# Row sums of the softmax: the two half sums added on VectorE for ten of sixteen head pairs, and the division moved one pair later

## The chip, the cores and the metric

One NeuronCore of a Trainium2 chip runs the whole program in one launch. The metric is the device time of one execution in microseconds (us). The kernel before took 799.79 us (median of three runs, 799.49 to 800.53). Below, PE is TensorE, DVE is VectorE, ACT is ScalarE, POOL is GpSimd and SP is SyncE.

## What is computed

Attention with cluster routing feeds an MLP mixer. There are 4 batches, 8 heads, 768 tokens and a head width of 64. A query sees only the keys that fall in the same of 16 clusters:

```python
mask = q_assign[:, :, :, None] == k_assign[:, :, None, :]
scores = np.where(mask, scale * (q @ k.T), -1e9)
attn = np.exp(scores - max(scores))
attn = attn / (np.sum(attn, axis=-1, keepdims=True) + 1e-09)
x = attn @ v                                    # then heads side by side: (4, 768, 512)
h = np.maximum(xt @ w_tok1, 0.0) @ w_tok2       # over tokens, xt = x transposed
u = x + h.transpose(0, 2, 1)
h2 = np.maximum(u @ w_ch1, 0.0) @ w_ch2         # over channels
return u + h2
```

The change concerns the sum in the fourth line and the division by it.

## The kernel before

All arithmetic is fp32. The kernel runs three stages one after the other.

**Attention** goes over 16 units; unit (or pair) `m` is two heads of one batch, `b, hp = divmod(m, 4)`. In each unit PE does, in the order in which `pair` (L1283) calls for it:

- `scores(m)`: twelve chunks. A chunk is 128 keys by 384 queries for both heads; it fills two PSUM banks, and the chunks use the bank pairs 0-1, 2-3 and 4-5 in turn. The mask is added as a second, bf16 matmul. ACT takes the exponential of each chunk (L1191) into one of seven buffers `exs`; a unit uses six, one for each block of 128 keys.
- `values(m, i)` for the six key blocks: exponentials times V, in 32 matmul instructions each, summed up in banks 6 and 7.
- `route(m + 2, 0)` before `values(m, 4)`: cluster scores of the unit after next, into bank 0. DVE turns them (L1086), takes maxima, compares and turns them back (L1091); ACT makes the mask rows of it (L1095).
- `sums(m, 5)` before the last `values`: a matmul with a matrix of ones adds the exponentials over the keys. Its two passes `n` read `es[0]` and `es[1]` and add up in bank 5.

DVE has made `es[0]` and `es[1]` at the end of `scores`: each is the sum of three exponential buffers, in two additions of 128x1536 elements (`tt`, L881). After the unit, `finish_x` (L1247) turns the denominators out of bank 5 (L1250), clips them (L1252), takes the reciprocal (L1259), turns the result out of banks 6 and 7 into `x` (L1264) and multiplies `x` by the reciprocals (L881, 128x768).

Beside this, DVE prepares the mixer's weights in 31 pieces (`weight_round`, L1307, five instructions each; and the combinations `sub1`, `sub2` after every second piece). The pieces are needed only later and are fitted in where DVE has room. ACT also splits q and k into halves for a DMA transpose and joins them (L871).

**The token stage** multiplies by `w_tok1` and `w_tok2`; ACT copies and DMA transposes bring `x` into the layout `u` (`x_into_u`). **The channel stage** multiplies by `w_ch1` and `w_ch2` for two groups of two batches; each step of three matmuls is followed by an addition out of PSUM on DVE.

The order of the work is made when the program is built. `Program.add` records every operation with what it reads and writes. `Program.plan` then hands operations to the engines by assumed costs (`COST`, and numbers at each call) and due times that are counted back from the PE order. PE's own order is the order of the calls; the other engines' orders come out of the plan. On the chip each engine runs its list in that fixed order and waits on semaphores.

Of the kernel before, what the change touches and what calls it, by code (L numbers as in the profile page):

```python
# [14 lines left out]
ALU = mybir.AluOpType  # L15
# [3 lines left out]
B, H, S, D = 4, 8, 768, 64  # L19
C = 16  # L20
P = 128
NJ = S // P
# [8 lines left out]
HS = HJ * P  # L31
# [14 lines left out]
NP = NG // 2  # L46
NU = 2 * NP
W = 64
SUM_LO, SUM_HI = 1e-15, 1e15
GRAIN = 32  # L50

COST = {
    "ACT": (0.09, 0.00083),
# [175 lines left out]
class Buf:  # L229
# [17 lines left out]
    def k(self, *parts):  # L247

        out = []
        for lo, hi in parts or ((0, self.words),):  # L250
            out.extend(range((self.off + lo) // GRAIN, -(-(self.off + hi) // GRAIN)))
        return out
# [467 lines left out]
def kernel(  # L720
# [26 lines left out]
    nc = tc.nc  # L747
    g = Program()
# [4 lines left out]
    ps = res.enter_context(tc.tile_pool(name="ps", bufs=1, space=bass.MemoryType.PSUM)).tile(  # L753
        [P, 8, 512], F32, name="ps"
    )
# [9 lines left out]
    def buf(kb, shape, dt=F32):  # L765
        return Buf(arena, int(kb * 256), shape, dt)
# [24 lines left out]
    es = [buf(84 + 6 * i, [2, S]) for i in range(2)]  # L791
# [44 lines left out]
    def bank(*i):  # L836
        return [("ps", n) for n in i]


    def mm(dst, lhsT, rhs, start, stop, cost, rd, wr, pos=None, tr=None):  # L840
        def fn(e):
            nc.tensor.matmul(  # L842
                dst, lhsT=lhsT, rhs=rhs, start=start, stop=stop, tile_position=pos,
                is_transpose=tr, skip_group_check=True,
            )

        return g.add({"PE": cost}, fn, rd, wr, mode=(lhsT.shape[0], lhsT.shape[1]))
# [6 lines left out]
    def cost(kind, n):  # L854
        a, b = COST[kind]
        return a + b * n
# [22 lines left out]
    def tt(dst, a, b, op, n, rd, wr, engines=("DVE",)):  # L879
        def fn(e):  # L880
            (nc.vector if e == "DVE" else nc.gpsimd).tensor_tensor(out=dst, in0=a, in1=b, op=op)  # L881

        return g.add({e: cost(e, n) for e in engines}, fn, rd, wr)
# [10 lines left out]
    def vec(fn, c, rd, wr, early=0.0):  # L894
        return g.add({"DVE": c - 0.08}, lambda e: fn(), rd, wr, early=early)
# [27 lines left out]
    def load_qkr(m, after=0.0):  # L923
        b, hp = divmod(m, H // 2)
        for i, a in ((0, k), (1, q)):
            dma(
                qkr.ap[:, i].rearrange("p h j d -> p h (j d)"),
                a[b, 2 * hp : 2 * hp + 2].rearrange("h (p j) d -> p h (j d)", p=P),
                [], qkr.rows(i, i + 1), 384, 1536, after,
            )  # L930
# [96 lines left out]
    def turn_qk(m, banks):  # L1027
        src, T = qks[m % 2], Ts[m % 3]
        for n, bk in enumerate(banks):
            for i in range(4):  # L1030
                a, j = divmod(4 * n + i, NJ)
                a = 1 - a
                turn(
                    ps[:, bk, i * P : (i + 1) * P],
                    src.ap[:, a, j].rearrange("p h d -> p (h d)"),
                    [("qk", m % 2, a, 0), ("qk", m % 2, a, 1)] + src.rows(a, a + 1), bank(bk),
                )

            copy(
                T.ap[:, 4 * n : 4 * n + 4].rearrange("p a t -> p (a t)"), ps[:, bk], 512,  # L1040
                bank(bk), T.rows(4 * n, 4 * n + 4),
            )
# [103 lines left out]
    unit = {}  # L1146

    def scores(m):
        nonlocal nex
        T, M = Ts[m % 3], Ms[m % 2] if m else M0  # L1150
        st = unit[m] = [exs[(nex + i) % len(exs)] for i in range(NJ)]
        nex += NJ

        def chunk(n):
            return divmod(n, NJ) if m == 0 else divmod(n, 2)[::-1]

        def plain(n):
            u, i = chunk(n)
            s, r0 = n % 3, NJ + HJ * u
            for h in range(2):  # L1160
                hs = slice(64 * h, 64 * h + 64)
                mm(
                    ps[:, 2 * s + h, 0:HS], T.ap[hs, i],
                    T.ap[hs, r0 : r0 + HJ].rearrange("p a t -> p (a t)"), True, False, 0.3225,
                    T.rows(i, i + 1) + T.rows(r0, r0 + HJ), bank(2 * s + h), pos=(64 * h, 0),
                )

        ahead = 3 if m == 0 else 0
        for n in range(ahead):
            plain(n)  # L1170
        if m == 0:
            turn_qk(1, (7, 6, 7))
            load_qkr(3, 26.0)
            route(1, 6)
        for n in range(2 * NJ):
            u, i = chunk(n)
            s = n % 3
            if n >= ahead:
                plain(n)
            for h in range(2):  # L1180
                hs = slice(64 * h, 64 * h + 64)
                mm(
                    ps[:, 2 * s + h, 0:HS], M.ap[hs, 1, i * P : (i + 1) * P],
                    M.ap[hs, 0, u * HS : (u + 1) * HS], False, True, 0.081,
                    [("mask", m % 2, a, c, h) for a, c in ((1, i // HJ), (0, u))] + M.k(),
                    bank(2 * s + h), pos=(64 * h, 0),
                )
            ex = st[i]
            g.add(
                {"ACT": 0.70},  # L1190
                lambda e, ex=ex, s=s, u=u: nc.scalar.activation(  # L1191
                    out=ex.ap[:, :, u * HS : (u + 1) * HS], in_=ps[:, 2 * s : 2 * s + 2, 0:HS],
                    func=ACT.Exp, scale=SM_SCALE,
                ),
                bank(2 * s, 2 * s + 1),
                ex.rows(0, 2, u * HS, (u + 1) * HS) + ([("exps", m)] if n == 2 * NJ - 1 else []),
            )
        for n in range(2):
            a = es[n]
            x, y, z = st[HJ * n : HJ * n + HJ]  # L1200
            tt(a.ap, x.ap, y.ap, ALU.add, 2 * S, x.k() + y.k(), a.k())
            tt(a.ap, a.ap, z.ap, ALU.add, 2 * S, a.k() + z.k(), a.k())

    def mms(parts, cost, rd, wr, mode):

# [9 lines left out]
    def tokens(ap, gr):  # L1215

        return ap.rearrange("p (j t) -> p j t", t=P)[:, :, 32 * gr : 32 * gr + 32]
# [13 lines left out]
        )  # L1231

    def sums(m, bk):
        for n in range(2):
            mms(
                [
                    (
                        ps[32 * gr : 32 * gr + 32, bk, 0:HS], ones.ap,
                        tokens(es[n].ap.rearrange("p h t -> p (h t)"), gr), n == 0, n == 1,
                        (0, 32 * gr),  # L1240
                    )
                    for gr in range(4)
                ],
                0.645, es[n].k() + ones.k(), bank(bk), (P, 32),
            )

    def finish_x(m, bk):  # L1247
        b, hp = divmod(m, H // 2)
        x, rcp = xs[b], rcps[m % 2]
        vec(lambda: nc.vector.transpose(out=denT.ap, in_=ps[:, bk, 0:HS]), 0.57, bank(bk), denT.k())  # L1250
        def den():
            nc.vector.tensor_scalar(  # L1252
                out=dall.ap[:, m].rearrange("p h j -> p (h j)"),
                in0=denT.ap.rearrange("p (n r) -> p n r", r=32)[:, :, 0],
                scalar1=SUM_LO / 2, scalar2=2 * SUM_HI, op0=ALU.max, op1=ALU.min,
            )

        vec(den, 0.2, denT.k(), [("dall", m)])
        vec(lambda: nc.vector.reciprocal(out=rcp.ap, in_=dall.ap[:, m]), 0.2,  # L1259
            [("dall", m)], rcp.k())  # L1260
        cols = slice(hp * P, (hp + 1) * P)
        xk = x.rows(0, NJ, hp * P, (hp + 1) * P)
        vec(
            lambda: nc.vector.transpose(  # L1264
                out=x.ap[:, :, cols].rearrange("p j (c d) -> p c j d", d=32),
                in_=ps[:, 6:8, 0:HS],
            ),
            0.96, bank(6, 7), xk,
        )
        xv = x.ap[:, :, cols].rearrange("p j (h d) -> p j h d", h=2)  # L1270
        tt(
            xv, xv,
            rcp.ap.rearrange("p h j -> p j h").unsqueeze(3).to_broadcast([P, NJ, 2, D]),
            ALU.mult, S, xk + rcp.k(), xk,
        )
# [7 lines left out]
    def pair(m):  # L1283
        scores(m)
        if m >= 1 and m + 2 < NP:
            join_qk(m + 2)
        if m:
            next_qk(m)
        for i in range(NJ):
            if i == 4 and 1 <= m < NP - 2:  # L1290
                route(m + 2, 0)
            if i == NJ - 1:
                sums(m, 5)
            values(m, i)
        finish_x(m, 5)
        if m == 0:
            load_v(2)
            turn_qk(2, (1, 2, 3))
            route(2, 0)
            next_qk(m)  # L1300
        if m + 3 < NP:
            load_v(m + 3)
# [632 lines left out]
    first = token1(0, Tx, w1)  # L1935
# [71 lines left out]
```

## Time and profile before

| | |
|---|---|
| three runs | 799.49, 799.79, 800.53 us; median 799.79 us |
| the profiled execution | 799.38 us; its span from first to last instruction 797.6 us |
| granted TensorE clock | 0.999 of full speed |
| PE busy | 783.8 us (98% of the span) |
| DVE busy | 659.4 us (83%) |
| ACT busy | 469.8 us (59%) |
| POOL busy | 188.8 us (24%) |

How to read it: the attention units fill the span up to about 333 us, the token stage lies between about 333 and 419 us, and the channel stage takes the rest. A row of the timeline names the start in us from the span's start, the length, engine, line and operation, output and input shape, and how many equal neighbours it merges; a bracket gives the idle time of that engine just before and what ended it. In the groups, `x80` is the number of instructions, then come the busy time in us and the mean length of one in ns. A matmul's end is modelled, so for PE the distance between starts says more than the length. In the windows, the columns are busy us of PE, PEld (weight loads), DVE, ACT and POOL with their instructions, the granted clock, the busy share of the DMA engines and GB/s.

### The profile page before, as it was taken

The page shows a single profiled execution, that of the slowest core. Times are in us where ns is not written, and L with a number is a line of the kernel's source. Part 1 is how long each engine was busy: PE and PEld are TensorE (multiplying, and loading weights), DVE is VectorE, ACT ScalarE, POOL GpSimd, SP SyncE. Part 2 cuts the span into 40 slices and gives each one's busy share as a digit, 9 for nine tenths or more (in the row PEclk, how much of TensorE's full clock was granted, in tenths as well). Part 3 has the DMA queues.
Part 4 walks back from the last instruction along what each step waited for, and adds up shares of the span by engine and source line. Part 5 has one row for each costly group of instructions (what it writes and reads, how often), then busy time and mean ns, then how long its engine had stood idle before and what let it go on. Part 6 is the DMA issues. An engine that isn't in the chain of part 4 may idle for free.

```text
span 797.6 us, 15467 instructions
## 1 busy us (share of the span) xinstructions
PE 783.8 (98%) x6063; PEld 466.9 (59%) x6063; DVE 659.4 (83%) x861; ACT 469.8 (59%) x618; POOL 188.8 (24%) x184
## 2 busy tenths in 40 slices
PE   7999999999999999999999999999999999999997
PEld 5566666666666666544555555555555555555554
DVE  6988899999999999999994677899952566799964
ACT  5588888888888875698714568503256104400433
POOL 0000000000000000000353499800186379840000
PEclk9999999999999999999999999999999999999999
DMA  9466779999999985479848787635597433333766
GB/s 213 153 160 167 172 169 229 223 211 215 229 226 237 223 249 134 97 148 211 177 122 274 270 290 265 223 99 144 143 210 195 130 106 102 99 104 105 177 148 154
DMA packets 264881, 143.69 MB, mean 180 GB/s; under 512 B 184160, under 2 KB 260704, under 8 KB 264800
## 3 DMA queue, kind: packets, MB, share of 16 engines
q1 hardware_dynamic: 262432, 141.83, 70.2%
q8 instruction: 50, 0.82, 0.4%
q10 hardware_dynamic: 2368, 0.79, 0.4%
q14 instruction: 31, 0.25, 0.1%
HBM read 91.95 MB, written 28.61 MB: 151 GB/s over the span
## 4 chain that ended last, share of the span: by engine, by line
PE 82%; DVE 11%; ACT 4%; issue 2%; ACTq 0%; DVEq 0%
PE ps L842 65%; PE ps L1208 17%; DVE arena L881 9%; ACT arena L871 3%; ACT arena L861 1%; ACT arena L888 0%; DVE arena L863 0%; DVE arena L1264 0%; DVE arena L1337 0%; ACTq L901 0%; ACT L980 0%; ACT arena L1191 0%; DVE arena L1334 0%; DVE arena L1331 0%; DVE arena L1086 0%
## 5 line engine op out<-in xcount | busy, mean ns | idle before, releaser
L842 PE MATMUL ps<-arena 128*128 128x384 f32 (+5 forms) x2735 | 639.7, 462 | 8.4 <-DVE arena L881 2.1
L842 PEld LDWEIGHTS ps<-arena 128*128 128x128 f32 (+1 forms) x2351 | 341.1, 184 | 252.0 <-issue 62.7
L881 DVE TENSOR_TENSOR arena<-arena 128x1536 f32<-128x1536 f32 (+6 forms) x341 | 354.8, 1063 | 19.8 <-ACT arena L1191 9.0
L881 POOL TENSOR_TENSOR arena<-arena 128x384 f32<-128x384 f32 x178 | 188.1, 1086 | 516.5 <-DVE arena L881 382.4
L881 DVE TENSOR_TENSOR arena<-ps,arena 128x384 f32<-128x384 f32 (+3 forms) x227 | 189.3, 844 | 100.2 <-PE ps L842 90.4
L871 ACT COPY arena<-arena 128x768 uint16<-128x768 uint16 x223 | 192.0, 952 | 58.7 <-DVE arena L881 29.3
L1191 ACT ACTIVATE arena<-ps 128x768 f32<-128x768 f32 x192 | 153.8, 810 | 30.4 <-PE ps L842 29.3
L1208 PE MATMUL ps<-arena 128*32 128x192 f32 (+1 forms) x3328 | 151.1, 339 | 0.0
L1208 PEld LDWEIGHTS ps<-arena 128*32 128x32 f32 x3328 | 106.5, 110 | 48.0 <-issue 18.3
L861 ACT COPY arena<-ps 128x1152 f32<-128x1152 f32 (+2 forms) x45 | 32.8, 738 | 133.7 <-PE ps L842 125.2
L888 ACT ACTIVATE arena<-arena 128x1152 f32<-128x1152 f32 (+1 forms) x38 | 40.0, 1077 | 55.8 <-DVE arena L881 55.3
L1865 ACT ACTIVATE arena<-arena 128x768 f32<-128x768 f32 x40 | 38.5, 967 | 17.3 <-DMA arena<-in_moe_w_ch_dram 17.0
L842 PEld LDWEIGHTS <-arena 64*128 64x128 bf16 x384 | 19.2, 94 | 25.0 <-issue 0.6
L1095 ACT ACTIVATE arena<-arena 128x384 bf16<-128x384 f32 x16 | 11.3, 707 | 16.3 <-issue 9.9
L1331 DVE SCALAR_TENSOR_TENSOR arena<-arena 128x512 uint32<-128x512 uint32 (+1 forms) x31 | 20.5, 667 | 0.5
L1337 DVE SCALAR_TENSOR_TENSOR arena<-arena 128x512 f32<-128x512 uint32 (+1 forms) x31 | 20.3, 666 | 0.5
L1264 DVE STREAM_TRANSPOSE arena<-ps 128x768 f32<-128x768 f32 x16 | 15.6, 974 | 0.6 <-PE ps L1208 0.4
L1327 DVE TENSOR_SCALAR arena<-arena 128x512 uint32<-128x512 uint32 (+1 forms) x31 | 12.6, 406 | 0.3 <-DMA arena<-in_moe_w_ch_dram 0.3
L1334 DVE TENSOR_SCALAR arena<-arena 128x512 uint32<-128x512 uint32 (+1 forms) x31 | 12.3, 409 | 0.4
L1086 DVE STREAM_TRANSPOSE arena<-ps 128x384 f32<-128x384 f32 x16 | 9.2, 575 | 3.0 <-PE ps L842 2.7
L1250 DVE STREAM_TRANSPOSE arena<-ps 128x384 f32<-128x384 f32 x16 | 9.2, 575 | 0.8 <-PE ps L1208 0.6
L1091 DVE STREAM_TRANSPOSE arena<-arena 128x384 f32<-128x384 f32 x16 | 9.3, 578 | 0.6
(58 smaller groups left out, 47.2 us busy)
## 6 DMA issues: line engine op xcount, KB each, us to landing
arena<-wd SPq DMA_DIRECT2D x196, 192.0 KB, 2.4
wd<-arena SPq DMA_DIRECT2D x84, 224.0 KB, 3.6
arena<-in_moe_w_ch_dram SPq DMA_DIRECT2D x48, 256.0 KB, 4.6
arena<-in_moe_w_ch_dram SPq DMA_DIRECT2D x16, 768.0 KB, 5.3
arena<-in_v_dram SPq DMA_DIRECT2D x16, 384.0 KB, 4.8
out_dram<-arena SPq DMA_DIRECT2D x14, 384.0 KB, 4.1
arena<-in_k_dram SPq DMA_DIRECT2D x13, 384.0 KB, 4.0
arena<-in_q_dram SPq DMA_DIRECT2D x13, 384.0 KB, 4.4
```

What stands on the lines that cost most here:

```text
L842: nc.tensor.matmul(dst, lhsT=lhsT, rhs=rhs, start=start, stop=stop, tile_position=pos, is_transpose=tr, skip_group_check=True,)
L861: nc.scalar.copy(out=dst, in_=src)
L871: nc.scalar.copy(out=dst, in_=src)
L881: (nc.vector if e == "DVE" else nc.gpsimd).tensor_tensor(out=dst, in0=a, in1=b, op=op)
L888: nc.scalar.activation(out=dst, in_=src, func=ACT.Relu)
L1191: lambda e, ex=ex, s=s, u=u: nc.scalar.activation(out=ex.ap[:, :, u * HS : (u + 1) * HS], in_=ps[:, 2 * s : 2 * s + 2, 0:HS], func=ACT.Exp ...
L1208: nc.tensor.matmul(dst, lhsT=lhsT, rhs=rhs, start=start, stop=stop, tile_position=pos, skip_group_check=True,)
L1264: lambda: nc.vector.transpose(out=x.ap[:, :, cols].rearrange("p j (c d) -> p c j d", d=32), in_=ps[:, 6:8, 0:HS],),
L1327: vec(lambda: nc.vector.tensor_scalar(out=hh, in0=hi, scalar1=0x07FFFFFF, scalar2=3, op0=ALU.bitwise_and, op1=ALU.logical_shift_left,), f, ...
L1331: vec(lambda: nc.vector.scalar_tensor_tensor(out=TT, in0=hi, scalar=0xC0000000, in1=hh, op0=ALU.bitwise_and, op1=ALU.bitwise_or), 0.14 + 0 ...
L1337: vec(lambda: nc.vector.scalar_tensor_tensor(out=ll, in0=lo, scalar=float(2.0**-52), in1=hh.bitcast(F32), op0=ALU.mult, op1=ALU.mult,), 0. ...
L1865: lambda e, i=i, func=func, bias=bias, n=n, hi=hi: nc.scalar.activation(out=hi, in_=hi, func=func, bias=bias, accum_out=wsum.ap[:, i, n : ...
```

## The change

For the units 1 to 10 (the letters V of `FOLD`) DVE adds `es[0]` to `es[1]` in a fifth addition, and PE multiplies only this one sum by the ones. The other six units keep both halves. The multiplication with ones and the division move for all units: `sums(m - 1)` is now called after `values(m, 0)` of the next unit, with the denominators' part of `finish_x` (turning, clipping, reciprocal, multiplying `x`) behind it. Turning `x` out of banks 6 and 7 stays at the unit's end. The additions `add_up(m)` are called behind `sums(m - 1)`, because they overwrite what that reads. The last unit does both at its end, into bank 4. The branch for `"T"` isn't used.

```diff
+FOLD = "-VVVVVVVVVV-----"
...
+    def add_up(m):
+        st = unit[m]
         for n in range(2):
             a = es[n]
             x, y, z = st[HJ * n : HJ * n + HJ]
             tt(a.ap, x.ap, y.ap, ALU.add, 2 * S, x.k() + y.k(), a.k())
             tt(a.ap, a.ap, z.ap, ALU.add, 2 * S, a.k() + z.k(), a.k())
+        a, b = es[1], es[0]
+        if FOLD[m] == "V":
+            tt(a.ap, a.ap, b.ap, ALU.add, 2 * S, a.k() + b.k(), a.k())
...
     def sums(m, bk):
-        for n in range(2):
+        first = 0 if FOLD[m] == "-" else 1
+        for n in range(first, 2):
...
-                        tokens(es[n].ap.rearrange("p h t -> p (h t)"), gr), n == 0, n == 1,
+                        tokens(es[n].ap.rearrange("p h t -> p (h t)"), gr), n == first, n == 1,
...
-    def finish_x(m, bk):
+    def finish_x(m, bk, part):
...
+        if part == 0:
+            vec(  # transpose of banks 6 and 7 into x
...
+            return
...
         for i in range(NJ):
             if i == 4 and 1 <= m < NP - 2:
                 route(m + 2, 0)
-            if i == NJ - 1:
-                sums(m, 5)
+            if i == 1:
+                if m:
+                    sums(m - 1, 5)
+                    finish_x(m - 1, 5, 1)
+                add_up(m)
+            if i == NJ - 1 and m == NP - 1:
+                sums(m, 4)
             values(m, i)
-        finish_x(m, 5)
+        finish_x(m, 5, 0)
+        if m == NP - 1:
+            finish_x(m, 4, 1)
```

More of the change, by code (lines that the diff above doesn't have):

```diff
@@ L1202, in scores, with fn @@
             tt(a.ap, a.ap, z.ap, ALU.add, 2 * S, a.k() + z.k(), a.k())
+        a, b = es[1], es[0]
+        if FOLD[m] == "V":
+            tt(a.ap, a.ap, b.ap, ALU.add, 2 * S, a.k() + b.k(), a.k())
+        if FOLD[m] != "T":
+            return
+        def fn(e):
+            nc.gpsimd.dma_start(
+                a.ap.rearrange("p h t -> p (h t)"), b.ap.rearrange("p h t -> p (h t)"),
+                accum_op=ALU.add,
+            )
+        g.add({"POOL": 1.0}, fn, a.k() + b.k(), a.k(), (2.2 * 768 * 1024, 6144))
     def mms(parts, cost, rd, wr, mode):
@@ L1245, in sums @@
             )
-    def finish_x(m, bk):
+    def finish_x(m, bk, part):
         b, hp = divmod(m, H // 2)
         x, rcp = xs[b], rcps[m % 2]
+        cols = slice(hp * P, (hp + 1) * P)
+        xk = x.rows(0, NJ, hp * P, (hp + 1) * P)
+        if part == 0:
+            vec(
+                lambda: nc.vector.transpose(
+                    out=x.ap[:, :, cols].rearrange("p j (c d) -> p c j d", d=32),
+                    in_=ps[:, 6:8, 0:HS],
+                ),
+                0.96, bank(6, 7), xk,
+            )
+            return
         vec(lambda: nc.vector.transpose(out=denT.ap, in_=ps[:, bk, 0:HS]), 0.57, bank(bk), denT.k())
@@ L1260, in finish_x @@
             [("dall", m)], rcp.k())
[L1261 to L1269, printed above, removed]
         xv = x.ap[:, :, cols].rearrange("p j (h d) -> p j h d", h=2)
```

## The prediction

> **What bounds the kernel now.** I read the page's first part, then the windows by stage, then the waits, then the timeline of one attention unit.
>
> ```profile
> PE 783.8 (98%) x6063; PEld 466.9 (59%) x6063; DVE 659.4 (83%) x861; ACT 469.8 (59%) x618; POOL 188.8 (24%) x184
> ...
> core 0: us, PE busy (x) PEld busy (x) DVE busy (x) ACT busy (x) POOL busy (x), PEclk, DMA share, GB/s
> 20.00:340.00 320.00, 318.51 (x4585) 198.39 (x4582) 298.25 (x412) 258.10 (x335) 0.00 (x0) 1.00 0.81 193
> 340.00:420.00 80.00, 77.74 (x213) 39.05 (x212) 75.24 (x134) 55.88 (x71) 20.16 (x19) 1.00 0.78 167
> 420.00:520.00 100.00, 100.00 (x312) 58.84 (x311) 67.88 (x60) 62.66 (x101) 70.41 (x68) 1.00 0.77 262
> ...
> PE ps L842 <- DVE arena L881: 2.1, 5, 0.9
> ```
>
> In the attention PE is busy for 318.5 of 320 us, but DVE for 298.3 too: two engines stand at their limit, and the change moves work from one to the other. The waits decide which leads: PE waited for a DVE addition five times in the whole span, 2.1 us together. The unit confirms it.
>
> ```profile
> 176.13 9.96 PE L842 MATMUL ps<-arena 64*128 64x384 f32 x72
> 177.25 9.75 ACT L1191 ACTIVATE arena<-ps 128x768 f32<-128x768 f32 x12 [1.57 <-PE ps L842]
> 186.02 5.41 PE L1208 MATMUL ps<-arena 128*32 128x192 f32 x128
> 191.25 0.83 PE L842 MATMUL ps<-arena 128*32 128x384 f32 x8
> 191.89 4.07 PE L1208 MATMUL ps<-arena 128*32 128x192 f32 x80
> 194.61 0.71 ACT L1095 ACTIVATE arena<-arena 128x384 bf16<-128x384 f32 x1 [0.97 <-ACT arena L871]
> 194.73 0.58 DVE L1250 STREAM_TRANSPOSE arena<-ps 128x384 f32<-128x384 f32 x1 [0.20 <-PE ps L1208]
> 195.89 1.40 PE L842 MATMUL ps<-arena 64*128 64x384 f32 x8
> ```
>
> From start to start: scores 9.89 us, four `values` 5.23 (1.31 each), the route 0.64, then `values`, sums, `values`, and the next unit begins 19.76 us after this one. So PE sets the time, and a PE instruction taken out of a unit counts, if DVE still arrives in time.
>
> **PE's part, the gain.** A half sum has the shape of the route: eight instructions of 32 columns by 384. The route takes 0.64 us from start to start (191.25 to 191.89).
>
> ```profile
> L1208 PE MATMUL ps<-arena 128*32 128x384 f32 x256 | 23.6, 486 | 0.0
> L881 DVE TENSOR_TENSOR arena<-arena 128x1536 f32<-128x1536 f32 x80 | 140.0, 1756 | 13.0 <-ACT arena L1191 9.0 <-DVE arena L881 0.5
> L1331 DVE SCALAR_TENSOR_TENSOR arena<-arena 128x512 uint32<-128x512 uint32 x27 | 18.3, 683 | 0.3
> L1327 DVE TENSOR_SCALAR arena<-arena 128x512 uint32<-128x512 uint32 x27 | 11.2, 414 | 0.3 <-DMA arena<-in_moe_w_ch_dram 0.3
> ```
>
> The 256 instructions are sixteen units of two halves; ten halves go: 10 x 0.64 = **-6.4 us**.
>
> **DVE's part, what is added.** Ten additions of 1.756 us are 17.6 us on an engine that idled 21.7 us in those 320. Work has to give way: in the built order of the changed kernel the weight instructions behind the attention grow from 49 to 70. Does a unit then fit? The fixed work per unit:
>
> ```profile
> 172.42 0.58 DVE L1086 STREAM_TRANSPOSE arena<-ps 128x384 f32<-128x384 f32 x1
> 173.03 0.55 DVE L1087 TENSOR_REDUCE arena<-arena 128x24 f32<-128x384 f32 x1
> 173.62 0.56 DVE L881 TENSOR_TENSOR arena<-arena 128x384 f32<-128x384 f32 x1
> 174.21 0.58 DVE L1091 STREAM_TRANSPOSE arena<-arena 128x384 f32<-128x384 f32 x1
> 174.97 0.58 DVE L1250 STREAM_TRANSPOSE arena<-ps 128x384 f32<-128x384 f32 x1 [0.18 <-PE ps L1208]
> 175.58 0.17 DVE L1252 TENSOR_SCALAR arena<-arena 128x12 f32<-128x12 f32 x1
> 175.79 0.23 DVE L1259 RECIPROCAL arena<-arena 128x12 f32<-128x12 f32 x1
> 175.94 0.63 DVE L1331 SCALAR_TENSOR_TENSOR arena<-arena 128x512 uint32<-128x512 uint32 x1
> 176.48 0.97 DVE L1264 STREAM_TRANSPOSE arena<-ps 128x768 f32<-128x768 f32 x1
> 177.49 0.96 DVE L881 TENSOR_TENSOR arena<-arena 128x768 f32<-128x768 f32 x1
> ```
>
> Route 2.27, finish 2.91, five additions 8.78: 13.96 us. The order puts eight to twelve weight instructions between two routes in units 5 to 11, about ten (fourteen to sixteen before). A piece has two instructions of 0.414, two of 0.683 and an addition that I take like those: 0.58 on average, 5.8 for ten, 19.8 us of durations. Neighbours that don't depend on each other overlap: 175.94 plus 0.63 reaches past 176.48 by 0.09. With ten such pairs 18.9 us remain, against 19.76 - 0.64 = 19.12 on PE. It fits, by 0.2 us.
>
> *The place where DVE could hold PE.* The next unit's scores need bank 0, so the route's first turn must have ended. The order puts in front of it: turning the last unit's denominators, the two additions of `es[1]` (they wait for the sums, whose input they overwrite) and the fold. From the start of the half sum: 0.64, plus 0.26 until DVE starts (sums end at 191.89 + 1.31 + 1.28 = 194.48, DVE starts at 194.73), 0.58, three times 1.756, then the turn 0.58: 7.3 us. PE needs 0.64, three `values` 3.92, route 0.64, two `values` 2.62: 7.8. So 0.5 us of room, less up to 0.68 where a weight instruction stands in between: nothing in units 5 to 11.
>
> Unit 2 is fuller: ten weight instructions and seven large additions, since unit 1's came late. 12.3 + 2.27 + 1.7 (two turns and a clip) + 5.8 - 0.9 = 21.2 us against 19.12, an overhang of 2.1. It starts from a lead: in unit 1 the turn ends after 0.64 + 0.26 + 0.58 + 3 x 1.756 + 0.58 = 7.3 us, and PE needs it after 1.28 + 3.92 + 0.64 + 2.62 = 8.5. So PE waits **+1.0**; bounds 0 and 2.5 (no lead, and the next unit late as well).
>
> **A move the diff doesn't show.** In units 3 to 11 ACT's mask operation (L1095) now stands between the eighth and the ninth exponential; before it stood ahead of all twelve (194.61). Unit 1 of the kernel before has it after the ninth:
>
> ```profile
> 36.23 0.85 PE L842 MATMUL ps<-arena 128*32 128x384 f32 x8 [0.78 <-ACT arena L861]
> ...
> 37.79 9.96 PE L842 MATMUL ps<-arena 64*128 64x384 f32 x72 [0.71 <-DVE arena L1086]
> 38.98 7.19 ACT L1191 ACTIVATE arena<-ps 128x768 f32<-128x768 f32 x9
> 46.07 0.70 ACT L1095 ACTIVATE arena<-arena 128x384 bf16<-128x384 f32 x1
> 46.76 2.24 ACT L1191 ACTIVATE arena<-ps 128x768 f32<-128x768 f32 x3
> 47.68 5.41 PE L1208 MATMUL ps<-arena 128*32 128x192 f32 x128
> ```
>
> There PE went from scores to values in 9.89 us as ever: free. One place earlier, the ninth exponential moves from about 45.4 to 46.05 and ends at 46.9; the twelfth chunk, which needs its banks, would begin at 37.79 + 11 x 0.81 = 46.7. That is 0.2 us, in nine units **+1.8**; bounds 0 and 0.7 each (the whole operation), 6.2.
>
> **Ends.** The third copy of `turn_qk(2)` goes from ACT to DVE, which shortens the 0.78 us that PE waits at 36.23: **-0.3** (0 to -0.6). In the last unit all four additions must follow `sums(14)`: 0.64 + 0.26 + 4 x 1.756 = 7.9 us, and the last half sum is due after 1.28 + 4 x 1.31 + 0.64 = 7.2: **+0.8** (0.3 to 1.6). Multiplying `x` a unit later costs nothing: units 0 to 14 have a unit of cover, and in the last unit the order keeps it where it was.
>
> **Behind the attention.** The token stage begins when the exponentials' buffers are free, and its chain runs over ACT and DVE, so it moves with the attention's end:
>
> ```profile
> 336.31 5.76 ACT L871 COPY arena<-arena 128x768 uint16<-128x768 uint16 x7
> ```
>
> DVE has two more additions of 1.756 and a second finish to do at its start, and ten weight instructions less in all: **+0.3** (-0.5 to +2). Thirty-five weight instructions now stand in the first channel products, where there were four:
>
> ```profile
> 454.66 1.36 DVE L881 TENSOR_TENSOR arena<-ps,arena 128x1152 f32<-128x1152 f32 x1 [0.58 <-PE ps L842]
> ```
>
> An eviction takes 1.36 us and 0.58 are idle, so one instruction of 0.41 to 0.68 fits into most gaps: **0** (up to +3, a tenth of a microsecond for each of the 31 new ones; the gap is the cover).
>
> Sum: -6.4 + 1.0 + 1.8 - 0.3 + 0.8 + 0.3 = **-2.8 us**. From the profiled execution's own 799.38 us (1.8 of them outside the span) this gives 796.6; the median of the three runs, 799.79, lies 0.4 above that execution, so beside the median I predict 797.0.
>
> [...] By the row, PE has 318.5 of 320 us, and its period never waits. [...]
>
> **The rivals.**
>
> 1. *DVE takes the lead* (slower). If the ten weight instructions don't overlap as in the trace, a unit is 19.8 of DVE plus the 0.26 at the handover, 20.06, and more than 19.76 is slower than before: ten units x 0.3 = +3.0, with the tail's 0.8 and the 0.3 behind it 803.9 beside the median. For it: the room of only 0.2 us; against: before, some 28 instructions with the same overlaps ran in 19.76 without a wait. Chance 0.13.
> 2. *The gain is kept whole up to the tail*: the mask operation finds its gap and DVE is on time: 799.8 - 6.4 + 0.8 = 794.2. Chance 0.15.
> 3. *Given back behind the attention*: the weight work pushed out of the attention lands where PE waits. If half of the 35 instructions, each 0.2 too long for its gap, hold an eviction, the channel loses 3.5 us: 797.0 + 3.5 = 800.5. [...] Chance 0.22, a third of it for a loss beyond 801.4.
> 4. *The fold isn't done*: excluded, the ten additions stand in the built order.
>
> **Chances.** The forecast case (795 to 798.2) 0.5, rival 2 0.15, rival 3 0.22, rival 1 0.13. A measurement of this kernel tells a change of about 0.2% (1.6 us) from none: below 798.2 is faster, above 801.4 slower. Faster: 0.50 + 0.15 = 0.65. Same: two thirds of rival 3, 0.15. Slower: the rest of it and rival 1, 0.20. The range goes from 793.3 (rival 2 with the first pair's gain and a little more) to 802.0, which takes in most of rival 3 and leaves out rival 1.
>
> **What would show it.** Right: units 2 to 11 with a period of 19.1 to 19.4 us; L1208 with ten times eight matmuls of 384 columns fewer; ninety 128x1536 additions; a wait of PE for L1191 of about 0.2 us a unit; DVE at 19 of 20 us in the attention. Wrong: a period near 20 with PE waiting for L881 or L1086 (rival 1), or new PE waits between 409 and 460 us (rival 3).

## The result: slower by 1.1%, and the profile after

The changed kernel takes 809.06 us (median; 807.96 to 809.6), the kernel before 800.16 us beside it; the ratio is 1.0111, 95% interval [1.0099, 1.0123]. The forecast was 797.0 us. The profiled execution took 808.78 us with a span of 807.0, against 799.38 and 797.6 before: 9.4 us more. Three of the 84 runs of the kernel before that were taken beside the experiments needed 807.4 to 808.5 us, two of them with a granted clock of 0.994 like the 0.993 of the changed kernel here; no trace of these was kept, so why is open. In the changed kernel most lines are higher by one; the multiplication of the values is L1225 (was L1208), the addition helper L882, the mask operation L1096.

**The attention** did what was predicted. First the groups of the attention, then one unit on PE and ACT, and that unit as a window (columns: busy us of PE, PEld, DVE, ACT, POOL, granted clock, DMA share, GB/s):

```profile
L882 DVE TENSOR_TENSOR arena<-arena 128x1536 f32<-128x1536 f32 x76 | 132.2, 1747 | 11.4 <-PE ps L1225 8.2 <-ACT arena L1192 1.0
L1225 PE MATMUL ps<-arena 128*32 128x384 f32 x176 | 17.4, 487 | 0.5 <-DVE arena L882 0.5
...
172.81 10.16 PE L843 MATMUL ps<-arena 64*128 64x384 f32 x72
173.93 6.52 ACT L1192 ACTIVATE arena<-ps 128x768 f32<-128x768 f32 x8 [2.67 <-PE ps L843]
180.35 0.70 ACT L1096 ACTIVATE arena<-arena 128x384 bf16<-128x384 f32 x1
181.04 2.90 ACT L1192 ACTIVATE arena<-ps 128x768 f32<-128x768 f32 x4
182.90 6.05 PE L1225 MATMUL ps<-arena 128*32 128x192 f32 x136
192.13 10.16 PE L843 MATMUL ps<-arena 64*128 64x384 f32 x72
...
172.81:192.13 19.32, 19.32 (x285) 12.03 (x281) 18.31 (x24) 16.53 (x22) 0.00 (x0) 1.00 0.74 192
```

There are 176 matmuls of 384 columns in place of 256. The unit has 19.32 us in place of 19.76: the half sum's 0.64 is gone, but the scores last 10.09 (172.81 to 182.90) in place of 9.89, because the mask operation now stands between the eighth exponential and the ninth. The end of the attention, and PE's waits from 20 to 330 us and behind that:

```profile
318.60 8.64 PE L1225 MATMUL ps<-arena 128*32 128x192 f32 x184
327.71 2.15 PE L1225 MATMUL ps<-arena 128*32 128x384 f32 x40 [0.47 <-DVE arena L882]
329.80 2.41 PE L843 MATMUL ps<-arena 128*128 128x512 f32 x5
...
PE ps L843 <- DVE arena L864: 0.9, 1, 0.9
PE ps L1225 <- DVE arena L882: 0.5, 1, 0.5
...
PE ps L843 <- issue: 7.6, 1, 7.6
PE ps L843 <- DVE arena L882: 2.2, 4, 1.2
```

The first matmul of the token stage starts at 329.80 us; before it was 332.95. So 3.15 us were won there. From then on I compared the start of the same matmul in both traces, after minus before: -3.5 us at the end of the token stage (419), -3.1 at 447, -2.7 at 462, **+5.1** behind a stall, +7.0 some 4 us later, +7.3 at the last products, and +9.4 at the end of the span. Two places took everything back.

**The stall.** It stands in the first channel products. DVE, POOL and PE there, then the windows (the same columns, PE's granted clock third from the end):

```profile
469.35 1.36 DVE L882 TENSOR_TENSOR arena<-ps,arena 128x1152 f32<-128x1152 f32 x1 [0.58 <-PE ps L843]
470.62 8.83 DVE L882 TENSOR_TENSOR arena<-arena 128x448 f32<-128x448 f32 x1
479.37 2.61 DVE L882 TENSOR_TENSOR arena<-ps,arena 128x1152 f32<-128x1152 f32 x2
...
451.43 27.54 POOL L882 TENSOR_TENSOR arena<-arena 128x384 f32<-128x384 f32 x28 [2.58 <-DVE arena L882]
...
480.82 19.46 PE L843 MATMUL ps<-arena 128*128 128x384 f32 x54 [7.64 <-issue]
...
473.18:477.64 4.46, 0.00 (x0) 0.00 (x0) 4.46 (x1) 0.00 (x0) 4.46 (x6) 1.00 0.05 19
477.64:480.82 3.18, 0.00 (x0) 0.03 (x1) 3.18 (x3) 0.07 (x1) 1.33 (x2) 0.50 0.13 29
480.82:484.47 3.65, 3.65 (x6) 2.12 (x7) 1.16 (x1) 3.65 (x5) 0.00 (x0) 0.50 0.50 112
484.47:490.00 5.53, 5.53 (x18) 3.24 (x18) 3.94 (x3) 4.29 (x6) 1.96 (x2) 1.00 0.61 207
```

One weight combination of 128x448 (`sub2`), which takes 0.62 us in another place (experiment 1), stands on DVE as busy for 8.83 us. It began while POOL ran 28 additions without a gap, and ended 0.5 us after POOL's run did (451.43 + 27.54 = 478.97). The evictions queue behind the combination, and PE stands for 7.64 us. "issue" names nothing there: the wait is for DVE, as the evictions at 479.37 show. The first of these ends at 480.7 (1.34 us), and PE resumes at 480.82. The granted clock falls to 0.50 while PE stands, 4.46 us after its last matmul, and stays there for 3.65 us after PE has resumed. In the kernel before, POOL had a run like it at this place, but DVE had only evictions beside it, each with one input from PSUM, and these weren't disturbed: 1.358 us on average, against 1.357 over the whole span. POOL's row there, and DVE's one group between 454 and 483 us:

```profile
454.16 28.92 POOL L881 TENSOR_TENSOR arena<-arena 128x384 f32<-128x384 f32 x30 [2.26 <-DVE arena L881]
...
L881 DVE TENSOR_TENSOR arena<-ps,arena 128x1152 f32<-128x1152 f32 x16 | 21.7, 1358 | 9.3 <-PE ps L842 9.3
```

**The end of the program.** Behind the last store SP runs a chain of semaphore and drain instructions. The views leave these out; in the trace's records SP stands still in this chain behind its 990th instruction:

```
kernel           SP records   hold in the closing chain that isn't common to all
before              988       none
after               996       1.92 us, behind no. 990
```

The hold accounts for the last 2 us. A transfer of an instruction queue lands in it; but these queues carry ten packets in the last 26 us of the kernel before too, so this alone doesn't show that the transfer is the cause.

### The profile page after: what moved, and what is told of

Same layout as the page of the kernel before. It is cut to its first block, busy times and chain, and to the rows that moved or that the text cites. A ratio compares the mean times of both kernels' runs of the same rounds, so it can differ in the third digit from the quotient of the medians.

```text
span 807.0 us, 15286 instructions
## 1 busy us (share of the span) xinstructions
PE 783.0 (97%) x5983; PEld 465.2 (58%) x5983; DVE 683.9 (85%) x871; ACT 464.7 (58%) x617; POOL 190.4 (24%) x185
## 4 chain that ended last, share of the span: by engine, by line
PE 80%; DVE 10%; ACT 3%; POOL 3%; issue 2%; DVEq 0%; POOLq 0%
PE ps L843 63%; PE ps L1225 17%; DVE arena L882 9%; POOL arena L882 3%; ACT arena L872 3%; ACT arena L862 0%; DVE arena L864 0%; ACT arena L889 0%; DVE arena L1362 0%; DVE arena L1359 0%; DVE arena L1365 0%; ACT arena L1192 0%; DVE arena L1355 0%; DVE arena L1087 0%; POOL arena masks.py:199 0%
## 5 line engine op out<-in xcount | busy, mean ns | idle before, releaser
L882 DVE TENSOR_TENSOR arena<-arena 128x1536 f32<-128x1536 f32 (+6 forms) x350 | 381.0, 1111 | 17.4 <-PE ps L1225 8.2
L882 POOL TENSOR_TENSOR arena<-arena 128x384 f32<-128x384 f32 x179 | 189.7, 1091 | 522.2 <-DVE arena L882 386.4
L882 DVE TENSOR_TENSOR arena<-ps,arena 128x384 f32<-128x384 f32 (+3 forms) x227 | 189.1, 845 | 84.1 <-PE ps L843 80.9
L1192 ACT ACTIVATE arena<-ps 128x768 f32<-128x768 f32 x192 | 150.5, 811 | 36.1 <-PE ps L843 34.5
L1225 PE MATMUL ps<-arena 128*32 128x192 f32 (+1 forms) x3248 | 144.9, 335 | 0.5 <-DVE arena L882 0.5
L1225 PEld LDWEIGHTS ps<-arena 128*32 128x32 f32 x3248 | 103.7, 110 | 45.2 <-issue 13.9
L1096 ACT ACTIVATE arena<-arena 128x384 bf16<-128x384 f32 x16 | 11.2, 701 | 12.0 <-issue 12.0
```

The lines of the kernel that those rows point to most:

```text
L1192: lambda e, ex=ex, s=s, u=u: nc.scalar.activation(out=ex.ap[:, :, u * HS : (u + 1) * HS], in_=ps[:, 2 * s : 2 * s + 2, 0:HS], func=ACT.Exp ...
L1225: nc.tensor.matmul(dst, lhsT=lhsT, rhs=rhs, start=start, stop=stop, tile_position=pos, skip_group_check=True,)
```

## Experiments

All times of "before" are runs beside the kernel in question.

**1. Move the one addition ahead of POOL's run.** A list of moves is applied to the finished order, and an instruction whose inputs aren't there yet is held back:

```diff
+MOVES = [(("sub2", 2, 5, 2), ("sub2", 2, 5, 0))]
...
+        for name, behind in MOVES:
+            at = next(i for i, (o, e) in enumerate(order) if self.names.get(o) == name)
+            item = order.pop(at)
+            to = next(i for i, (o, e) in enumerate(order) if self.names.get(o) == behind)
+            order.insert(to + 1, item)
```

> The changed kernel with one VectorE instruction moved: the last-but-one combination of the last weight round (sub2(2), 128x448, both inputs in SBUF), which stood inside POOL's unbroken run and lasted 8.83 us, stands right behind the first combination of that round, ahead of POOL's run. All else keeps its order. Theory A (one addition with two SBUF inputs is starved by POOL's back-to-back run, and the evictions queue behind it): the addition lasts 0.6 to 1.2 us, the 7.64 us stall of PE at 475 goes, and with it the low clock behind it (some 2 us): 809.1 - 7.8 - 1.9 = 799.4, and 797.3 if the 1.9 us at the program's end go too. Rival B (the evictions or the stores are late for another reason, the weight work in this stage as such): PE still stalls in 460 to 480, 806 to 809.

Measured: 799.42 us, ratio 0.999 [0.998, 0.9999]. The chip gives 9.6 us back for the place of one instruction. The moved combination in its new place; then POOL's run, and PE's waits behind the attention:

```profile
449.83 0.62 DVE L901 TENSOR_TENSOR arena<-arena 128x448 f32<-128x448 f32 x1
...
451.79 29.56 POOL L901 TENSOR_TENSOR arena<-arena 128x384 f32<-128x384 f32 x30 [3.12 <-DVE arena L901]
...
PE ps L862 <- DVE arena L901: 2.2, 4, 1.2
PE ps L862 <- issue: 0.4, 1, 0.4
```

Rival B falls: the other weight instructions stay in this stage, and of PE's waits only 0.4 us are new there ("issue"). The 2 us at the end stay too (1.46 us of hold, again behind SP's 990th instruction), and with what the other weight instructions cost in the channel stage (1.7 us, see below) the attention's gain is just cancelled.

**2 and 3. Put such an instruction into the kernel before.** Same place, once with two SBUF inputs, once with one:

```diff
+        nc.vector.tensor_tensor(out=flat[:, 0:448], in0=flat[:, 512:960], in1=flat[:, 1024:1472], op=ALU.add)
```

```diff
+        nc.vector.reduce_max(out=flat[:, 0:14], in_=flat[:, 512:960].rearrange("p (n c) -> p n c", c=32), axis=AX.X)
```

> The kernel before with one instruction more: a 128x448 addition of two SBUF inputs into a dead buffer, on VectorE, behind the third eviction of the product with index 1 in the first channel products, in the middle of POOL's run of 30 instructions (454 to 483 us); nothing reads its result. Theory A: it lasts until POOL pauses, up to 9 to 12 us, the evictions behind it wait, PE stalls: 808 to 812. Rival B (the addition gets its turn at POOL's next instruction, as the one at 456.87 us of the changed kernel did in 1.15 us, and the harm there came from something else): 800.2 to 801.5.

> The kernel before with another instruction at the same place as in e2_two_inputs: a maximum over 128x448 of one SBUF input into 128x14 of a dead buffer; nothing reads it. Theory A, in the form that two SBUF inputs make the difference: 0.5 us for it, no stall, 800.2 to 800.8. Rival C (any VectorE instruction without a PSUM input is starved there): as long as e2_two_inputs, 808 or more.

Measured: 811.7 us, ratio 1.0145 [1.0128, 1.0162], for the addition; 800.32 us, 0.9998 [0.9978, 1.0018], for the maximum. DVE's rows around the addition with PE's wait, and then the row of the maximum:

```profile
470.24 1.36 DVE L883 TENSOR_TENSOR arena<-ps,arena 128x1152 f32<-128x1152 f32 x1 [0.58 <-PE ps L844]
471.51 10.11 DVE L1651 TENSOR_TENSOR arena<-arena 128x448 f32<-128x448 f32 x1
481.54 2.61 DVE L883 TENSOR_TENSOR arena<-ps,arena 128x1152 f32<-128x1152 f32 x2
...
482.94 9.43 PE L844 MATMUL ps<-arena 128*128 128x384 f32 x23 [8.87 <-DVE arena L883]
...
482.94:486.50 3.56, 3.56 (x6) 2.04 (x7) 1.21 (x1) 3.56 (x5) 0.00 (x0) 0.50 0.22 26
```

```profile
471.72 0.61 DVE L1651 TENSOR_REDUCE arena<-arena 128x14 f32<-128x448 f32 x1
```

One addition makes such a loss, 11.8 us of it, in a kernel without folds: 8.87 us of stall, and the granted clock at 0.50 for 3.56 us behind it. A maximum that reads one SBUF input in the same place is free. It differs from the addition in the operation and in how little it writes too, so the second input alone isn't isolated; and one input isn't safe by itself. In the changed kernel a weight instruction with one SBUF input, 0.42 us elsewhere, took 1.22 beside a single POOL addition, and another 1.00:

```profile
434.10 1.24 POOL L882 TENSOR_TENSOR arena<-arena 128x384 f32<-128x384 f32 x1 [3.33 <-PE ps L843]
434.40 1.22 DVE L1355 TENSOR_SCALAR arena<-arena 128x512 uint32<-128x512 uint32 x1
...
417.20 1.00 DVE L1362 TENSOR_SCALAR arena<-arena 128x512 uint32<-128x512 uint32 x1
```

**4. The deferral alone.** `FOLD = "-" * 16`.

> The changed kernel without a single half sum added on VectorE: all sixteen pairs keep both sums on TensorE, but sums, denominators and multiplication stand a unit later as in the changed kernel. The order puts no weight instruction into POOL's run. Theory A: the units have 19.76 us, no starved addition, 799.5 to 801.0. Rival D (the deferral itself costs in the attention, or shifts the tail and the end of the program): 802 or more; if the hold of 1.9 us at the program's end comes from the longer program text, it is here too, and the sum is 801.5 to 803.

Measured: 800.12 us, ratio 0.9999 [0.999, 1.0009]. One unit:

```profile
155.20 9.96 PE L843 MATMUL ps<-arena 64*128 64x384 f32 x72
165.09 6.70 PE L1225 MATMUL ps<-arena 128*32 128x192 f32 x144
174.97 1.40 PE L843 MATMUL ps<-arena 64*128 64x384 f32 x8
```

19.77 us, as before: adding up, multiplying and scaling one unit later costs nothing and brings nothing. SP has 987 records and no hold.

**5 and 6. The hold at the end.** SP gets drain instructions in the attention, 24 in the kernel of experiment 1, 8 in the kernel before:

```diff
+    def pad(self, e):
+        self.nsp += e == "SP"
+        if e == "SP" and 200 <= self.nsp < 200 + PAD:
+            self.extra()
...
+    g.extra = lambda: nc.sync.drain()
```

> The kernel of e1_ahead with 24 drain instructions more on SyncE, one behind each of its transfers 200 to 223, in the attention, where SyncE has room. Traces so far: in the changed kernel and in e1_ahead SyncE stands still for 1.9 and 1.5 us at the end of the program, both times behind its 990th instruction of the trace (of 996 and 995), with a transfer of instructions landing at that time; before and the others have 987 or 988 and no such hold. Theory E (the program has grown past a limit of what SyncE has at hand there): with 1019 the 990th lies ahead of the wait for the last stores, so the hold goes: 799.4 - 1.9 = 797.5. Rival F (the hold hangs on something else, the last stores or the shape of the tail): 799.0 to 799.8 as e1_ahead.

> The kernel before with 8 drain instructions more on SyncE, one behind each of its transfers 200 to 207, which makes 996 of them, as many as the changed kernel has. Theory E: a hold of about 1.9 us at the end of the program, 801.7 to 802.0. Rival F: 799.9 to 800.3.

Measured: 797.52 us, ratio 0.9965 [0.9951, 0.9979], and 801.75 us, ratio 1.002 [1.0011, 1.003]. SP's records:

```
kernel           SP records   hold in the closing chain
e1_ahead            995       1.46 us, behind no. 990
e5_pad24           1019       none
e6_before_pad8      996       2.23 us, behind no. 990
```

Theory E held in both directions, with the same position each time: the hold went and came with the number of SP's instructions, none at 988 and 1019, 1.46 to 2.23 us at 995 and 996. What ends the hold isn't shown. The change had lengthened SP's program by eight semaphore instructions, to 996; with its 988 the kernel before was two short of the 990th. With 1019, the 990th lies 13.5 us ahead of the end, where SP waits for stores anyway.

**7 and 10. The mask operation.** e7_mask has this line, e10_best the same with 11 in place of 8; both keep the move and the drains of e5_pad24:

```diff
+MOVES += [(("mask", m), ("exp", m - 1, 8)) for m in range(4, 13)]
```

> The kernel of e5_pad24 with ScalarE's mask operation of the pairs 4 to 12 placed behind the ninth exponential of the unit, where it stood before the change in unit 1, in place of between the eighth and the ninth. Theory G (the operation there costs PE 0.2 us a unit): units 3 to 11 have 19.12 us in place of 19.31, 1.7 us less than e5_pad24, 795.8 if that has 797.5. Rival H (the units are held by VectorE, 19 of whose 19.3 us are taken, and the wait only changes its name): less than 0.5 us.

> The kernel of e7_mask with the mask operation of the pairs 4 to 12 behind the twelfth exponential in place of the ninth, ahead of the copies for the next pair. In e7_mask the scores run without a wait (9.89 us), and the units still have 19.21 us and not 19.12. Theory I (the operation, wherever it stands among the exponentials, makes the last ones late for the values, by 0.09 us): 19.12 us a unit, 9 x 0.09 = 0.8 us less than e7_mask, 795.6. Rival H (VectorE holds the unit, or the copies behind it come late): 796.2 to 797, or slower.

Measured: 796.41 us, ratio 0.9951 [0.9935, 0.9968], and 795.98 us, ratio 0.9939 [0.9918, 0.9961]. The unit of the second:

```profile
171.09 9.96 PE L872 MATMUL ps<-arena 64*128 64x384 f32 x72
180.99 6.05 PE L1254 MATMUL ps<-arena 128*32 128x192 f32 x136
190.21 2.21 PE L872 MATMUL ps<-arena 64*128 64x384 f32 x14
```

Scores 9.90 us, unit 19.12: the 0.2 us belonged to the operation, not to DVE, and rival H falls. Behind the ninth exponential half of it came back (units of 19.21 us); behind the twelfth all of it. So e7_mask came 1.1 us below e5_pad24, where 1.7 were expected. e10_best is the fastest of all: the change with two places in the order mended and 24 drains on SP gains 0.6%. Between e7_mask and e10_best the medians differ by 0.4 us where 0.8 were expected, and the intervals overlap.

**8, 11 and 12. When does POOL let such an addition in?** The addition of experiment 2, seven and four evictions earlier, and then in its old place with a POOL instruction that reads its result and so makes POOL pause:

> The kernel before with the same 128x448 addition of two SBUF inputs as in e2_two_inputs, but seven evictions earlier, near the beginning of POOL's run (about 458 us), where POOL follows close behind the evictions that it needs. Theory A: it waits until POOL runs out of work that is ready; POOL's next pieces need evictions that queue behind it, so that comes after 2 to 8 us, and PE stalls by that less 1 us: 802 to 808. Rival B (its turn comes at the next end of a POOL instruction, as for the one at 456.87 us of the changed kernel, 1.15 us): 800.0 to 801.0.

> The kernel before with the 128x448 addition of two SBUF inputs behind the eviction that lies three behind that of e8_early (there it lasted 0.67 us and cost nothing) and four ahead of that of e2_two_inputs (there 10.1 us): at about 464 us, 10 us into POOL's run of 29. Theory J (it is starved where POOL's next pieces have all their inputs and stand ready one behind another, which is so from about 466 us on, when the products that POOL follows have been evicted): here it is still served after one instruction of POOL, 799.7 to 800.5. Rival K (only the first few instructions of POOL's run let it in, by chance): starved until POOL pauses, 15 us or until the evictions that POOL needs are held, 803 or more.

> The kernel of e2_two_inputs, where the 128x448 addition lasted 10.1 us, with one POOL instruction more: a 128x384 addition that reads the result, put behind the first POOL instruction that began after the other one was held (the first difference for the last product, 471.5 to 472.5 us). POOL so has to pause for VectorE one instruction later, in place of going on to 481 us; nothing of the reference reads either result. Theory A (VectorE waits for a pause of POOL and for nothing else): the addition lasts 1.2 to 1.8 us, the evictions behind it come 0.5 to 1 us late, 800.3 to 801.5. Rival L (the addition at that place is slow for a reason of its own, its buffers or a transfer that it waits for): 10 us again, and POOL held with it, 811 or more.

Measured: 799.8 us (ratio 0.9997 [0.9987, 1.0006]), 799.98 us (0.9996 [0.9976, 1.0016]) and 800.7 us (1.0 [0.9977, 1.0023]). The addition in the three, with the POOL instruction behind it in the first and POOL's rows in the last:

```profile
458.11 0.67 DVE L1651 TENSOR_TENSOR arena<-arena 128x448 f32<-128x448 f32 x1
458.25 1.39 POOL L883 TENSOR_TENSOR arena<-arena 128x384 f32<-128x384 f32 x1
```

```profile
463.91 0.63 DVE L1651 TENSOR_TENSOR arena<-arena 128x448 f32<-128x448 f32 x1
```

```profile
472.00 1.53 DVE L1651 TENSOR_TENSOR arena<-arena 128x448 f32<-128x448 f32 x1
...
454.74 18.31 POOL L883 TENSOR_TENSOR arena<-arena 128x384 f32<-128x384 f32 x19 [2.26 <-DVE arena L883]
473.61 1.01 POOL L1654 TENSOR_TENSOR arena<-arena 128x384 f32<-128x384 f32 x1 [0.56 <-DVE arena L1651]
```

My expectation for e8_early was wrong: near the start of the run the addition gets its turn at the next end of a POOL instruction, whose successor then takes 1.39 us in place of 1.0. At 464 us it is the same, as theory J said. At 472 it isn't, unless POOL has to pause: in e12_pool_waits POOL's run ends at 473.05 and the addition at 473.53. So what ended the wait in the late part is shown: a pause of POOL. Why POOL makes room without a pause up to 464 us and not from 470 on is not. Theory J forecast the result at 464 us, but no run isolates it, and POOL's own rows show no difference: its additions start 0.95 to 0.97 us apart ahead of the early additions as ahead of the late ones.

**9. Eight folds in place of ten**, nothing moved by hand: `FOLD = "-VVVVVVVV-------"`, with the 24 drains.

> The changed kernel with half sums added in eight pairs (1 to 8) in place of ten, and with the 24 drain instructions of e5_pad24; no instruction is moved by hand. With two additions less the last weight instruction stands ahead of POOL's run of itself. Theory A: no stall in the channel products; two half sums more on TensorE cost 2 x 0.45 = 0.9 us against e5_pad24, and fewer weight instructions between the evictions give some of the 1.2 us back that it lost there: 797.0 to 798.0. Rival B (the stall belongs to the folding as such): 804 or more.

Measured: 798.65 us, ratio 0.9974 [0.9955, 0.9993]. POOL's run is whole, and PE's waits name no stall:

```profile
451.71 29.01 POOL L890 TENSOR_TENSOR arena<-arena 128x384 f32<-128x384 f32 x30 [2.26 <-DVE arena L890]
...
PE ps L851 <- DVE arena L890: 1.9, 4, 0.8
```

Rival B falls again: eight folds have no stall. The time is 0.65 us above the expected range, and of the profiled execution 3.0 us lie outside its span where the other profiled ones have 1.8 to 2.0 (2.1 to 3.0 in its ten runs); I can't explain that, and whether eight or ten is better isn't told apart here.

## Why the prediction was wrong

The step that failed is the channel stage under "Behind the attention": "so one instruction of 0.41 to 0.68 fits into most gaps", with a term of 0, "up to +3". It measured +10.8. I took an instruction's length from rows where nothing competed with it, and asked only whether it fits into DVE's gap of 0.58 us. Experiments 1 and 2 show what the row beside it, POOL's unbroken 28.92 us, does to an instruction with two SBUF inputs: 10.1 us for 0.6. The other weight instructions stayed inside the bound: e5_pad24, without the stall, loses 1.7 us of its lead in the channel stage.

Rival 3 had the stage right (its sign named waits between 409 and 460 us; the stall begins at 473), and its price of 3.5 us was mis-sized, with the direction turned round: I priced what DVE's weight instructions do to the evictions; what happened is what POOL did to DVE. The trace of before has neighbours to price that by: seven between 391 and 418 us, additions with two SBUF inputs that were 0.4 to 0.8 us longer beside POOL's additions. Two of them, one that ran without POOL beside it, and POOL's rows:

```profile
391.73 1.42 DVE L881 TENSOR_TENSOR arena<-arena 128x512 f32<-128x512 f32 x1
399.72 0.68 DVE L881 TENSOR_TENSOR arena<-arena 128x512 f32<-128x512 f32 x1
414.22 1.31 DVE L881 TENSOR_TENSOR arena<-arena 128x448 f32<-128x448 f32 x1
...
390.33 2.28 POOL L881 TENSOR_TENSOR arena<-arena 128x384 f32<-128x384 f32 x2 [0.30 <-DVE arena L881]
413.62 4.09 POOL L881 TENSOR_TENSOR arena<-arena 128x384 f32<-128x384 f32 x3 [0.85 <-PE ps L842]
```

These rows showed the direction before the change was run: POOL held DVE (1.42 us in the first against 0.68 in the second, which ran alone). They wouldn't have given the size, since POOL's runs there are one to three instructions long, and the one of 28.92 us had no such addition in it.

Held were, in these traces, additions with two SBUF inputs (8.83 and 10.1 us, over nine and ten POOL instructions of 1.0 us) and two instructions with one SBUF input (1.22 and 1.00 us); the maximum (0.61 us) and the evictions (1.36 us) weren't. By what means POOL's run holds such an instruction, no trace shows.

The second miss is a term that I didn't have: 2 us at the end of the program. The hold came behind SP's 990th instruction in the three kernels in which that one lay in the closing chain. There SP's chain is all that is left to run (in the changed kernel the other engines' last records begin at 806.4 us, behind it), and the hold of 1.46 to 2.23 us adds to the time. Why it comes behind that instruction isn't shown.

The other steps, by their order in the prediction:

| step | predicted | measured |
|---|---|---|
| ten half sums | -6.4 | -6.4: 0.64 in each of units 2 to 11 |
| unit 2 overfull on DVE | +1.0 | 0: units 1 and 2 have 19.80 and 19.12 us |
| mask operation, units 3 to 11 | +1.8 | +1.7 (19.31 against 19.12) |
| first pair's third copy | -0.3 | +0.1: PE's wait for it is 0.88, was 0.78 |
| last unit's additions | +0.8 | +0.7: a wait of 0.47, and 0.2 more |
| token stage (to 419) | +0.3 | -0.3 |
| channel stage | 0 | +10.8, of which 9.1 with the starved addition |
| end of the program | none | +2.1 |

The attention's steps come to -3.9; the first scores of this execution began 0.75 us later than before, which leaves the 3.15 that I read off. That 0.75 belongs to the execution, not to the change: with the folds the scores begin between 10.0 us (e7_mask, e10_best) and 10.8, without them between 10.0 (before) and 10.6 (e12_pool_waits).

Without the two misses, in e5_pad24, the kernel takes 797.52 us, close to the forecast of 797.0. That is partly luck: the +1.0 for unit 2 didn't come, and the channel stage's 1.7 did.

For rival 1 (DVE takes the lead) nothing speaks: DVE was busy for 18.31 of a unit's 19.32 us and never late inside it.

## What to carry to other kernels

Before work is moved on to DVE, look in the trace at what POOL does at the time where that work, or the work that it pushes out, will land: a DVE instruction with two SBUF inputs in a long unbroken run of POOL cost here, in two places, not its own length but the time until POOL paused, 8.8 and 10.1 us, and in two others 0.63 and 0.67 us. One SBUF input was held too; the longest such wait seen here was 0.8 us (1.22 in place of 0.42), beside a single POOL instruction. Price it for the worst neighbour, not from rows where it ran alone; ordering it ahead of the run, or giving POOL a reason to pause, made it cheap again here (0.62 and 1.53 us). And where the last microseconds change without a reason in the work, count the instructions of the engine that closes the program: here a hold of 1.5 to 2.2 us came with seven or eight more of them on SP.

## What the runs showed of the hardware that I had not expected

- An addition of two SBUF inputs on DVE was held for 8.83 and 10.1 us by back-to-back POOL additions of 1.0 us each; a reduction of one SBUF input in the same place took 0.61 us, and evictions with one PSUM input 1.36, as ever. The same addition, earlier in the same run, was through in 0.63 and 0.67 us. A `tensor_scalar` of one SBUF input, 0.42 us elsewhere, took 1.22 and 1.00 beside a POOL addition.
- In stalls of 7.64 and 8.87 us PE's granted clock fell to 0.50 at 4.5 and 2.2 us after the last matmul, and stayed there for 3.65 and 3.56 us after PE resumed; of the 9.1 us that the starved addition cost in the channel stage, some 2 came behind the stall.
- SP stood still for 1.5 to 2.2 us behind the 990th instruction of its trace, in the three kernels in which that one lay in the closing chain; eight drain instructions in the middle of the program made the kernel before 0.2% slower, and 24 made another (e1_ahead) 0.24% faster.
